# Halves of three kinds of loads as issue entries of their own, and a new issue table, in a chunked recurrence with a feed-forward layer on one core

## The chip, the core and the metric

The kernel runs on one core of a Trainium2 chip. The core has five engines with instruction streams of their own: TensorE (PE, matmuls; its weight loads are shown as PEld), VectorE (DVE), ScalarE (ACT), GpSimd (POOL) and SyncE (SP), which here only issues DMA transfers. The metric is the device time of one execution in microseconds (us); the median of three executions is given.

## What is computed

For 4 batches and 8 heads a 40 x 40 state runs over 768 time steps; the outputs of all heads are joined to rows of 320 and go through a normalised two-layer feed-forward block.

```python
def _attn_ref(r, k, v, w, a, b):          # each (4, 8, 768, 40)
    for t in range(S):
        y[:, :, t] = einsum('bhd,bhde->bhe', rt, state)
        Sa = einsum('bhde,bhe->bhd', state, at)
        state_decay = state * wt[:, :, None, :] - einsum('bhd,bhe->bhde', Sa, bt)
        state = state_decay + einsum('bhd,bhe->bhde', vt, kt)

def _moe_ref(x, g_ln, w_ch1, w_ch2):      # x: (4, 768, 320)
    xn = (x - mean) / sqrt(var + 1e-06) * g_ln
    return x + maximum(xn @ w_ch1, 0.0) @ w_ch2
```

## The kernel before

The 768 steps are cut into 24 chunks of 32 steps (C = 32, NCH = 24). Within a chunk the recurrence is turned into matrix products; from chunk to chunk only the state is handed on. Two chunks make a group of the feed-forward block.

For each chunk c the kernel has these steps, named by the label `of` of their entry:

- `load0` (function load_e) loads w and a into the tile wa, of which there are two (c modulo 2); `load1` loads k and b into bk, of which there are seven.
- prep: scans over w on DVE make running products gE (label g, L213) and qE (label q, L222); aT is a times qE, in two halves (L231), on DVE or POOL; kb multiplies bk by gE in place (L246), on DVE or POOL; tri (L272) is a set of 16 products of bk and aT on PE, gk its signed copy (L278). aT and gk go to DRAM (d_a, d_g) and come back in other layouts as x2s.
- invert: the triangular matrices of a slab of two or four chunks are inverted in a row of small steps on DVE or POOL (yi, ytmp), and go through DRAM as d_tt to the tiles tt.
- chain: prh (L461), one or more solves with tt (L477) and st (L523), which makes the next state; DVE and ACT copy the results (x, hv, ub) between them. This is the sequence that runs from chunk to chunk.
- post: `rv` (function post_loads, L574) loads r and v into the tile rvu, of which there are two; ut transposes u on PE and ACT copies it into the same rvu (L592); z (L605) is a product of rvu with itself, y (L625) the output.
- ss (L555) transposes the state for y.
- After every second chunk, norm and moe for the group: l1 (L860), relu on ACT (hh, L865), its remainder on DVE (hl, L869), l2 (L837). Both layers use split-precision operands, three or more matmuls for each product.

No scheduler sets the order. The body only records entries ("tasks"), each with the keys that it reads and writes; a long string, TABLE, then lists their numbers in the order in which they are emitted, with the letter of the engine (p PE, d DVE, a ACT, g POOL, s SP) and, for those that need PSUM, the bank. Each engine runs its entries in that order, and waits at an entry until its data are there or its buffer is free. All DMA transfers are issued by SP, in the table's order, so an entry that waits on SP holds up all transfers behind it. A chunk from the third on is loaded in two halves of 48 partitions (RHALF), by two DMA instructions; in the kernel before, both belong to one entry.

The names that the change touches: load_e and its labels load0 and load1, post_loads and its label rv, the keys ("wa", i), ("bk", i) and ("rv", i) wherever they are read, and TABLE.

## Time and profile before

| | |
|---|---|
| median of three executions | 590.12 us (589.9 to 590.15) |
| the profiled execution | 590.2 us, of which 588.4 us are the span from its first to its last instruction |
| granted clock of PE, mean of what is recorded | 0.96 of full speed |
| busy: PE, DVE, ACT, POOL | 490.8, 420.1, 277.9, 200.5 us |
| read from and written to DRAM | 69.12 MB and 18.24 MB, 148 GB/s over the span |

The span is what the trace covers; 1.8 us of the execution lie around it. A busy time is the sum over the instructions of an engine, whatever limits the stage that they stand in.

### The profile page before, as it was taken

Reading aid. Unit: us, or ns where it says so; the run is one execution under the profiler, and the core shown is the slowest. Engines: PE = TensorE matmul, PEld = TensorE weight load, DVE = VectorE, ACT = ScalarE, POOL = GpSimd, SP = SyncE. Lnnn points to the kernel's source line nnn. Section 1 sums busy time; section 2 is a strip of 40 time slices with the busy share of each in tenths; the row PEclk is TensorE's granted clock in tenths of the full one; section 3 lists DMA queues with packets and bytes.
Section 4 is the critical chain, followed back from the end, with each engine's and each line's share of the span. In section 5 each row is a group of like instructions: output and inputs, shape, how many; then the busy total and the mean of one; then the engine's idle time right before and its main releaser. Section 6 shows DMA issues by size and latency. Waiting matters only on the chain.

```text
span 588.4 us, 24992 instructions
## 1 busy us (share of the span) xinstructions
PE 490.8 (83%) x10786; PEld 446.5 (76%) x10786; DVE 420.1 (71%) x908; ACT 277.9 (47%) x685; POOL 200.5 (34%) x284
## 2 busy tenths in 40 slices
PE   2540468789689889989997989599999999999996
PEld 2530367678579777988896979499999988989995
DVE  8687997788886879768787667477688865464531
ACT  8031745455346545444751555364435457453331
POOL 8433671247813462015523016445246400000000
PEclk9999999999889879989997989799999999999999
DMA  9999886658697699674994846668667747323000
GB/s 217 214 244 260 199 191 198 130 144 166 145 198 139 149 185 210 157 153 127 210 179 97 166 105 163 122 171 190 130 197 198 149 104 167 88 61 73 8 23 27
DMA packets 114387, 89.04 MB, mean 151 GB/s; under 512 B 83616, under 2 KB 94368, under 8 KB 114272
## 3 DMA queue, kind: packets, MB, share of 16 engines
q1 hardware_dynamic: 114272, 87.40, 64.5%
q8 instruction: 86, 1.41, 1.1%
q14 instruction: 29, 0.24, 0.1%
HBM read 69.12 MB, written 18.24 MB: 148 GB/s over the span
## 4 chain that ended last, share of the span: by engine, by line
PE 62%; DMA 14%; DVE 10%; issue 4%; ACT 3%; POOL 3%; SPq 3%; ACTq 0%; POOLq 0%; DVEq 0%
PE ps L860 18%; PE ps L837 17%; DMA wa<-in_et_dram 4%; PE ps L605 4%; DMA rvu<-in_rv_dram 4%; DMA bk<-in_et_dram 4%; PE ps L477 3%; PE ps L272 3%; PE ps L625 3%; PE ps L523 3%; PE ps L461 2%; PE ps L432 2%; PE ps L555 2%; DVE aT L231 2%; PE ps L586 1%
## 5 line engine op out<-in xcount | busy, mean ns | idle before, releaser
L837 PE MATMUL ps<-w,hh 128*128 128x320 f32 x480 | 118.9, 333 | 0.6 <-ACT xk L440 0.4
L860 PE MATMUL ps<-xh,w 128*128 128x256 f32 x480 | 110.4, 292 | 1.6 <-DVE w L751 1.0
L368 POOL TENSOR_TENSOR ytmp<-yi 128x198 f32<-128x198 f32 (+14 forms) x94 | 61.3, 652 | 93.1 <-DVE yi L372 83.2
L865 ACT ACTIVATE hh<-ps 128x256 fp32r<-128x256 f32 x120 | 45.5, 384 | 98.1 <-PE ps L860 92.1
L869 DVE SCALAR_TENSOR_TENSOR hl<-ps,hh 128x256 fp32r<-128x256 f32 x120 | 49.3, 419 | 54.1 <-ACT hh L865 53.3
L860 PEld LDWEIGHTS ps<-xh,w 128*128 128x128 f32 x480 | 84.4, 194 | 4.0 <-DVE w L751 1.3
L837 PEld LDWEIGHTS ps<-w,hh 128*128 128x128 f32 x480 | 79.8, 196 | 3.9 <-issue 0.5
L837 PE MATMUL ps<-w,hl 128*128 128x320 f32 x240 | 76.4, 318 | 0.0
L860 PE MATMUL ps<-xl,w 128*128 128x256 f32 x240 | 68.7, 286 | 0.0
L372 POOL TENSOR_TENSOR yi<-yi,ytmp 128x198 f32<-128x198 f32 (+19 forms) x104 | 58.8, 565 | 8.2
L231 POOL TENSOR_TENSOR aT<-wa,qE 48x512 f32<-48x512 f32 x23 | 28.4, 1236 | 72.2 <-PE ps L272 23.7
L440 ACT COPY xk<-ps 64x320 f32<-64x320 f32 x96 | 39.4, 419 | 20.8 <-PE ps L432 19.7
L837 PEld LDWEIGHTS ps<-w,hl 128*128 128x128 f32 x240 | 47.0, 196 | 0.1
L860 PEld LDWEIGHTS ps<-xl,w 128*128 128x128 f32 x240 | 46.6, 194 | 0.0
L272 PE MATMUL ps<-aT,bk 104*64 104x64 f32 x768 | 37.4, 271 | 9.0 <-ACT pi L263 5.7
L564 ACT COPY xk<-ps 40x320 f32<-40x320 f32 x92 | 38.4, 420 | 13.0 <-PE ps L555 11.8
L272 PEld LDWEIGHTS ps<-aT,bk 104*64 104x64 f32 x768 | 33.8, 181 | 12.6 <-issue 10.5
L613 DVE TENSOR_TENSOR x5s<-ps,mask 64x512 f32<-64x512 f32 x48 | 33.0, 687 | 14.1 <-PE ps L605 13.3
L213 DVE TENSOR_TENSOR_SCAN gE<-wa,start 112x528 f32<-112x528 f32 x24 | 30.4, 1267 | 14.6 <-DMA wa<-in_et_dram 14.5
L477 PEld LDWEIGHTS ps<-hv,tt 32*32 32x32 f32 (+1 forms) x1536 | 26.8, 121 | 14.8 <-issue 8.2
L508 ACT COPY x<-ps 32x320 f32<-32x320 f32 x62 | 25.9, 418 | 25.1 <-DVE x L508 13.8
L477 PE MATMUL ps<-hv,tt 32*32 32x40 f32 (+1 forms) x1536 | 30.3, 213 | 8.8 <-issue 3.1
(131 smaller groups left out, 1004.3 us busy)
## 6 DMA issues: line engine op xcount, KB each, us to landing
rvu<-in_rv_dram SPq DMA_DIRECT2D x48, 288.0 KB, 5.2
wa<-in_et_dram SPq DMA_DIRECT2D x44, 195.2 KB, 4.7
bk<-in_et_dram SPq DMA_DIRECT2D x44, 192.0 KB, 4.6
d_g<-gk SPq DMA_DIRECT2D x48, 128.0 KB, 3.1
x<-in_vt_dram SPq DMA_DIRECT2D x48, 128.0 KB, 3.6
d_a<-aT SPq DMA_DIRECT2D x48, 99.0 KB, 3.5
x2s<-d_a SPq DMA_DIRECT2D x48, 99.0 KB, 3.3
x5s<-in_r_dram SPq DMA_DIRECT2D x48, 96.0 KB, 3.1
```

The costliest lines, as they stand in the source:

```text
L231: (nc.gpsimd if e == "POOL" else nc.vector).tensor_tensor(out=a[rs, x, :, 0:256].rearrange("p x (i t) -> p i x t", t=C), in0=t[rs, 529:104 ...
L272: nc.tensor.matmul(banks[b[f"pg{c}"]][64 * pp:64 * pp + 64, 64 * i:64 * i + 64], lhsT=tb[R4, 64 * p:64 * p + 64], rhs=a[R4, :, pp, C * i:C ...
L368: g.tensor_tensor(out=tv, in0=y[:, j + 1:, j:j + 1].broadcast_to([n, m, j]), in1=y[:, j:j + 1, 0:j].broadcast_to([n, m, j]), op=ALU.mult)
L372: g.tensor_tensor(out=yv, in0=yv, in1=tv, op=ALU.add)
L440: nc.scalar.copy(out=xk[c % 2][zs, pp, :, hf], in_=banks[b[names[hf]]][zs, 0:CH].rearrange("p (j e) -> p j e", e=D))
L477: nc.tensor.matmul(o[xs, h], lhsT=lhs, rhs=vec[xs, h], start=True, stop=True)
L564: nc.scalar.copy(out=xk[i][bs, pp, par::2].rearrange("p h f e -> p f h e"), in_=banks[b[name]][64 * par:64 * par + D, 0:CH].rearrange("p ( ...
L613: nc.vector.tensor_tensor(out=x5s[zs, pp].rearrange("p f h t -> p (f h) t"), in0=banks[b[f"pz{c}"]][zs].rearrange("p (n t) -> p n t", t=C) ...
L837: nc.tensor.matmul(banks[b[name]][:, 0:CH], lhsT=l[:, us], rhs=ws[f"w2_{f}"][:, y], start=f == 0 and x == 0, stop=f == 9 and x == 2)
L860: nc.tensor.matmul(ph, lhsT=l, rhs=r, start=x == 0, stop=x == 7)
L865: nc.scalar.activation(out=hhs[n], in_=banks[b[name]][:, 0:256], func=AF.Relu)
L869: nc.vector.scalar_tensor_tensor(out=hls[n], in0=banks[b[name]][:, 0:256], scalar=0.0, in1=hhs[n].bitcast(F32), op0=ALU.max, op1=ALU.subtract)
```

## The change

Each half of a load of w and a, of k and b, and of r and v becomes an entry of its own, with a key of its own; whoever reads such a tile now names both halves. The loads of the first two chunks, which are made in one piece, stay one entry. The table is a new one throughout: it lists 2,669 entries in place of 2,601, in a new order, gives some of them to other engines (kb: 15 of 24 on DVE in place of 11; the halves of aT: 27 of 48 on POOL in place of 23), and takes other PSUM banks. The transfers are the same in number, size and address, and so are the matmuls.

```diff
     def load_e(c, part):
         t, cs, k = ((wa[c % 2], slice(0, 1041), ("wa", c % 2)), (bk[c % NBK], slice(1041, 2065), ("bk", c % NBK)))[part]
 
-        def emit():
-            for rs in RHALF if c > 1 else (R,):
-                sync.dma_start(out=t[rs], in_=et_in[c, rs, cs])
-        dma(emit, 380 if c > 1 else 430, w=[k], of=f"load{part}")
+        for x, rs in enumerate(RHALF if c > 1 else (R,)):
+            dma(lambda rs=rs: sync.dma_start(out=t[rs], in_=et_in[c, rs, cs]), 195 if c > 1 else 430,
+                w=[k + (x,)] + ([k + (1,)] if c < 2 else []), of=f"load{part}")
...
-        task("DVE", g_, 1.4, r=[kw, ks], w=[kg], of="g")
+        task("DVE", g_, 1.4, r=kws + [ks], w=[kg], of="g")
...
-        task("PE", tri, 0.75, r=[kbk, ("aT", c % 2, 0), ("aT", c % 2, 1)], bank=f"pg{c}", of="tri")
+        task("PE", tri, 0.75, r=kbs + [("aT", c % 2, 0), ("aT", c % 2, 1)], bank=f"pg{c}", of="tri")
...
-        def rv_():
-            for x, rs in enumerate(RHALF):
-                sync.dma_start(out=rvu[i][rs, 512 * x:512 * x + 1536], in_=rv[c, rs])
-        dma(rv_, 590, w=[("rv", i)], of="rv", land=3.0)
+        for x, rs in enumerate(RHALF):
+            dma(lambda x=x, rs=rs: sync.dma_start(out=rvu[i][rs, 512 * x:512 * x + 1536], in_=rv[c, rs]), 295,
+                w=[("rv", i, x)], of="rv", land=3.0)
...
-        task("ACT", vu_, 0.62, ps=[f"put{c}"], w=[("vu", i)], of="ut")
+        task("ACT", vu_, 0.62, r=[("rv", i, 0), ("rv", i, 1)], ps=[f"put{c}"], w=[("vu", i)], of="ut")
...
-        task("PE", z, 0.75, r=[("rv", i), ("vu", i)], bank=f"pz{c}", of="z")
+        task("PE", z, 0.75, r=[("rv", i, 0), ("rv", i, 1), ("vu", i)], bank=f"pz{c}", of="z")
...
 TABLE = """
-9d 26a 17g 29s 47s 22g 2d 30s 16a 99s 5d 96s 15g 3d 14d 516s 64d 28a 21g 48s 31d 4g 23g 10a 32d 33d 19g 18a 49d 6g 12a
+2d 13a 8g 29s 47s 0d 5d 99s 14d 4g 9d 20g 7g 311s 96s 31d 30s 312s 23g 32d 33d 22g 49d 38a 24g 526s 27a 527s 35d 510s
```

The first place is on SP, at the rv load of chunk 3 (tile rvu1); bk4 is the k and b load of a later chunk, wa1 a w and a load, r1 a weight load. Before:

```order
L194 DMA bk4_89<-in_et_dram 48x1024 x2
L578 DMA x5s_96<-in_r5_dram 48x512
L303 DMA d_g3_171<-gk_110 64x512 x2
L405 DMA x2_0_92<-in_vt_dram 32x1024
L578 DMA x5s_96<-in_r5_dram 48x512
L194 DMA wa1_84<-in_et_dram 48x1041 x2
L574 DMA rvu1_102<-in_rv_dram 48x1536 x2
```

and in the changed kernel:

```order
L304 DMA d_g3_171<-gk_110 64x512 x2
L193 DMA bk4_89<-in_et_dram 48x1024 x2
L663 DMA r1_0_3_1897<-in_w1_dram 128x256
L574 DMA rvu1_102<-in_rv_dram 48x1536
L193 DMA wa1_84<-in_et_dram 48x1041
```

The bk load now stands behind the d_g store, one half of the rv load stands behind bk and one weight load, and its other half stands some twenty rows further ahead, outside this piece; the wa load stands behind it in two entries.

The second place is on SP, at the rv load of chunk 14 (tile rvu0), from a tt load on; rvu1 is that of chunk 15, d_a21 a store of aT. Before:

```order
L398 DMA x2s_0_94<-d_a16_160 48x2x264
L310 DMA d_a21_165<-aT1_109 48x528 x2
L398 DMA x2s_0_94<-d_a16_160 48x2x264
L401 DMA x2s_1_95<-d_g4_172 32x2x256
L401 DMA x2s_0_94<-d_g5_173 32x2x256
L398 DMA x2s_1_95<-d_a15_159 48x2x264
L194 DMA wa1_84<-in_et_dram 48x1041 x2
L574 DMA rvu1_102<-in_rv_dram 48x1536 x2
L398 DMA x2s_1_95<-d_a15_159 48x2x264
L574 DMA rvu0_101<-in_rv_dram 48x1536 x2
L405 DMA x2_1_93<-in_vt_dram 32x1024
L194 DMA wa0_83<-in_et_dram 48x1041 x2
```

and in the changed kernel:

```order
L412 DMA tt0_115<-d_tt4_179 32x8x32 x4
L399 DMA x2s_0_94<-d_a16_160 48x2x264
L578 DMA x5s_96<-in_r5_dram 48x512
L412 DMA tt1_116<-d_tt4_179 32x8x32 x4
L574 DMA rvu0_101<-in_rv_dram 48x1536
L311 DMA d_a21_165<-aT1_109 48x528 x2
L574 DMA rvu0_101<-in_rv_dram 48x1536
L574 DMA rvu1_102<-in_rv_dram 48x1536
L578 DMA x5s_96<-in_r5_dram 48x512
L193 DMA wa0_83<-in_et_dram 48x1041
```

The two halves for chunk 14 now stand ahead of that for chunk 15. The load of wa1 stands further ahead, outside this piece, in two entries, and so do three of the x2s loads; the other two x2s loads come later.

The third place is on POOL, at the two kb products (line L246, L247 in the changed kernel) on bk5 and bk4, which follow a row of inversion steps. Before:

```order
L368 TENSOR_TENSOR ytmp0_113<-yi0_111 128x130
L372 TENSOR_TENSOR yi0_111<-yi0_111,ytmp0_113 128x5x26
L231 TENSOR_TENSOR aT0_108<-wa0_83,qE0_105 48x8x2x32
L246 TENSOR_TENSOR bk5_90<-bk5_90,gE1_104 112x1024
L246 TENSOR_TENSOR bk4_89<-bk4_89,gE0_103 112x1024
L336 MEMSET yi1_112 128x32
L368 TENSOR_TENSOR ytmp1_114<-yi1_112 128x30
L372 TENSOR_TENSOR yi1_112<-yi1_112,ytmp1_114 128x30
```

and in the changed kernel:

```order
L373 TENSOR_TENSOR yi0_111<-yi0_111,ytmp0_113 128x2x29
L369 TENSOR_TENSOR ytmp0_113<-yi0_111 128x30
L373 TENSOR_TENSOR yi0_111<-yi0_111,ytmp0_113 128x30
L232 TENSOR_TENSOR aT0_108<-wa0_83,qE0_105 48x8x2x32 x2
L247 TENSOR_TENSOR bk4_89<-bk4_89,gE0_103 112x1024
L337 MEMSET yi1_112 128x32
```

The product on bk5 is no longer on POOL (it is on DVE, some way ahead), and both halves of aT0 stand ahead of the one on bk4; before, one of these halves was on POOL and the other on DVE.

## Rows read from the trace of the kernel before

**Rows 1.** The page: busy us (share of the span) xinstructions of each engine.
```profile
PE 490.8 (83%) x10786; PEld 446.5 (76%) x10786; DVE 420.1 (71%) x908; ACT 277.9 (47%) x685; POOL 200.5 (34%) x284
```

**Rows 2.** Stages: length, busy of PE, PEld, DVE, ACT, POOL, clock, DMA share, GB/s.
```profile
0.00:60.00 60.00, 20.26 (x500) 17.56 (x500) 45.67 (x84) 20.64 (x37) 30.75 (x34) 1.00 0.93 233
...
136.00:156.50 20.50, 14.53 (x413) 12.75 (x412) 17.30 (x32) 9.62 (x26) 17.15 (x21) 0.99 0.77 174
...
136.00:380.00 244.00, 212.60 (x4923) 191.09 (x4924) 183.76 (x392) 120.24 (x303) 94.80 (x136) 0.91 0.73 158
...
380.00:550.00 170.00, 169.28 (x3965) 156.57 (x3963) 113.02 (x261) 85.94 (x219) 39.49 (x60) 1.00 0.56 134
```

**Rows 3.** PE's timeline: start, us, instruction, idle before it and its releaser.
```profile
157.04 1.98 PE L605 MATMUL ps<-rvu 104*64 104x64 f32 x32 [3.83 <-ACT rvu L592]
...
254.04 0.27 PE L477 MATMUL ps<-hv,tt 32*32 32x40 f32 x7 [1.71 <-issue]
...
314.95 1.30 PE L523 MATMUL ps<-x,xk 64*40 64x40 f32 x64 [4.26 <-ACT x L508]
...
376.26 0.92 PE L555 MATMUL ps<-ident,x 40*104 40x40 f32 x16 [6.79 <-ACT rvu L592]
```

**Rows 4.** Stages, as in rows 2: the stretches after three of the waits.
```profile
156.50:163.30 6.80, 6.01 (x119) 5.36 (x120) 6.21 (x13) 3.49 (x10) 3.52 (x7) 0.52 0.46 108
313.50:320.30 6.80, 5.35 (x82) 5.25 (x83) 3.60 (x8) 1.56 (x4) 0.00 (x0) 0.52 0.50 102
374.90:381.80 6.90, 5.54 (x86) 5.02 (x90) 2.92 (x6) 4.20 (x9) 0.10 (x1) 0.52 0.26 60
```

**Rows 5.** PE's timeline: two places before 136 us and one after.
```profile
111.42 1.98 PE L605 MATMUL ps<-rvu 104*64 104x64 f32 x32 [0.52 <-ACT rvu L592]
...
132.34 0.92 PE L523 MATMUL ps<-x,xk 64*40 64x40 f32 x21 [1.25 <-DVE x L508]
...
342.60 1.15 PE L605 MATMUL ps<-rvu 104*64 104x64 f32 x32
```

**Rows 6.** SP's timeline, 142 to 149 us: start, us, DMA issue, how many.
```profile
142.67 0.78 SPq L194 DMA_DIRECT2D bk<-in_et_dram  x2
...
148.99 0.89 SPq L574 DMA_DIRECT2D rvu<-in_rv_dram  x2
```

**Rows 7.** The chain that ended last: its pieces for two rv loads (start, us).
```profile
149.46 6.79 DMA rvu<-in_rv_dram
...
366.49 9.03 DMA rvu<-in_rv_dram
```

**Rows 8.** SP's timeline, 359 to 366 us.
```profile
359.05 0.39 SPq L398 DMA_DIRECT2D x2s<-d_a  x1
...
363.68 0.89 SPq L194 DMA_DIRECT2D wa<-in_et_dram  x2
...
366.02 2.18 SPq L574 DMA_DIRECT2D rvu<-in_rv_dram  x2
```

**Rows 9.** Stages, as in rows 2: 370 to 375 us.
```profile
370.00:375.00 5.00, 0.00 (x0) 0.00 (x0) 0.69 (x2) 0.00 (x0) 3.02 (x5) 0.96 1.04 192
```

**Rows 10.** The page's DMA issues: how many, KB each, median us to landing.
```profile
rvu<-in_rv_dram SPq DMA_DIRECT2D x48, 288.0 KB, 5.2
```

**Rows 11.** DVE's and POOL's timelines from 309 us.
```profile
309.00 4.93 DVE L231 TENSOR_TENSOR aT<-wa,qE 48x512 f32<-48x512 f32 x1
...
309.04 4.34 POOL L246 TENSOR_TENSOR bk<-bk,gE 112x1024 f32<-112x1024 f32 x2
```

**Rows 12.** Line L231: its instructions on DVE, duration in ns min/median/max.
```profile
L231 DVE TENSOR_TENSOR aT<-wa,qE x25: 651/690/4930, 9.7 to 403.4; 48x512 f32<-48x512 f32 x25
```

**Rows 13.** Groups by line on DVE: kb, busy us, mean ns, idle before.
```profile
L246 DVE TENSOR_TENSOR bk<-bk,gE 112x1024 f32<-112x1024 f32 x11 | 13.7, 1246 | 0.2
```

**Rows 14.** SP's and DVE's timelines in the start.
```profile
68.07 1.89 SPq L411 DMA_DIRECT2D tt<-d_tt  x4
...
57.61 1.26 DVE L213 TENSOR_TENSOR_SCAN gE<-wa,start 112x528 f32<-112x528 f32 x1 [3.64 <-DMA wa<-in_et_dram]
```

More of the change, by code (lines that the diff above doesn't have):

```diff
@@ L190, in load_e @@
         t, cs, k = ((wa[c % 2], slice(0, 1041), ("wa", c % 2)), (bk[c % NBK], slice(1041, 2065), ("bk", c % NBK)))[part]
-        def emit():
-            for rs in RHALF if c > 1 else (R,):
-                sync.dma_start(out=t[rs], in_=et_in[c, rs, cs])
-        dma(emit, 380 if c > 1 else 430, w=[k], of=f"load{part}")
+        for x, rs in enumerate(RHALF if c > 1 else (R,)):
+            dma(lambda rs=rs: sync.dma_start(out=t[rs], in_=et_in[c, rs, cs]), 195 if c > 1 else 430,
+                w=[k + (x,)] + ([k + (1,)] if c < 2 else []), of=f"load{part}")
     def prep(c):
         t, tb = wa[c % 2], bk[c % NBK]
-        kw, kbk = ("wa", c % 2), ("bk", c % NBK)
+        kws = [("wa", c % 2, x) for x in range(2)]
+        kbk = ("bk", c % NBK)
+        kbs = [kbk + (x,) for x in range(2)]
         n = 528
@@ L224, in q_ @@
                 initial=0.0, op0=ALU.mult, op1=ALU.max)
-        task("DVE", q_, 1.31, r=[kw, "last"], w=[kq], of="q")
+        task("DVE", q_, 1.31, r=kws + ["last"], w=[kq], of="q")
         a = aT[c % 2]
@@ L234, in a_ @@
                     in1=qe[rs, :, 1:33].rearrange("p (i x) t -> p i x t", x=2), op=ALU.mult)
-            task([("DVE", 0.68), ("POOL", 1.18)], a_, r=[kw, kq], w=[("aT", c % 2, x)], of="aT")
+            task([("DVE", 0.68), ("POOL", 1.18)], a_, r=kws + [kq], w=[("aT", c % 2, x)], of="aT")
         if c < 2 or c in FRAME:
@@ L247, in kb_ @@
                 out=kb, in0=kb, in1=ge[R, :, 0:C].unsqueeze(2).broadcast_to([112, 16, 2, C]), op=ALU.mult)
-        task([("DVE", 1.25), ("POOL", 2.2)], kb_, r=[kg], w=[kbk], of="kb")
+        task([("DVE", 1.25), ("POOL", 2.2)], kb_, r=[kg], w=kbs, of="kb")
         def qd_(e, b):
@@ L434, in pe @@
                         identity=ident[rs, rs])
-        task("PE", pe, 0.65, r=[("bk", c % NBK), "ident"], bank=names, of="kbt")
+        task("PE", pe, 0.65, r=[("bk", c % NBK, x) for x in range(2)] + ["ident"], bank=names, of="kbt")
         for hf in range(2):
@@ L927, in setup @@
         for i in range(2, NBK):
-            clear(bk[i][32:64], [("bk", i)], ("POOL",))
+            clear(bk[i][32:64], [("bk", i, 0), ("bk", i, 1)], ("POOL",))
         clear(ub, ["ub"])
@@ L931, in setup @@
         for i in range(2):
-            clear(rvu[i], [("rv", i), ("vu", i)])
+            clear(rvu[i], [("rv", i, 0), ("rv", i, 1), ("vu", i)])
     setup()
@@ L946, in range_check @@
     def range_check():
-        key = ("bk", NCH % NBK)
+        key = ("bk", NCH % NBK, 0)
+        both = [key, ("bk", NCH % NBK, 1)]
         acc = bk[NCH % NBK]
@@ L953, in zero @@
             (nc.gpsimd if e == "POOL" else nc.vector).memset(v, 0)
-        task([("POOL", 1.0), ("DVE", 0.6)], zero, w=[key], of="wz")
+        task([("POOL", 1.0), ("DVE", 0.6)], zero, w=both, of="wz")
         for i in range(8):
             t = wa[i % 2]
-            dma(lambda i=i, t=t: sync.dma_start(out=t[:, 0:n], in_=ww[i]), 492, w=[("wa", i % 2)], of="ww")
+            dma(lambda i=i, t=t: sync.dma_start(out=t[:, 0:n], in_=ww[i]), 492, w=[("wa", i % 2, 0), ("wa", i % 2, 1)], of="ww")
             def wild(e, b, t=t):
@@ L962, in wild @@
                     op0=ALU.bitwise_xor, op1=ALU.bitwise_or)
-            task("DVE", wild, 1.2, r=[("wa", i % 2)], w=[key], of="wild")
+            task("DVE", wild, 1.2, r=[("wa", i % 2, 0), ("wa", i % 2, 1)], w=[key], of="wild")
         def fold(e, b):
@@ L1202 @@
[L1202 to L1205 removed]
+2d 13a 8g 29s 47s 0d 5d 99s 14d 4g 9d 20g 7g 311s 96s 31d 30s 312s 23g 32d 33d 22g 49d 38a 24g 526s 27a 527s 35d 510s
+6g 34d 21g 50d 309s 97a 39p0 51d 36a 131a1 54a 64g 295s 37d 28a 310s 48s 10g 53d 41p2 52d 19a 292s 16a 293s 91p34 42d
@@ new lines @@
+781d 1009g 779a 1352d 985a 784p 1338d 680p5 879s 679p7 788d 1345s 685p 786d 1010g 787d 773s 881s 785d 986p4 801s
+1342p1 1353d 987a 968a 686p4 798a 1369d 1339a 803p2 1343d 1355g 1386a 804a 1370d 899p31 682a 1354d 805p2 900a 1371d
+1382s 791a 886p0 1057s 880s 806d 1011g 887a 1344s 807d 888p0 884s 1373d 684p 890a 1383s 808p2 1012d 901a 891a 1013d
+893a 911s 1356a 912s 913p3 683d 687a 1014g 1364s 809d 892a 689p 903a 812d 690p 1029s 889a 904p62 1015d 1028s 902a
+1056s 696p0 1016d 905a 1385s 914a 1384s 1372d 908a 915p1 1387d 906a 907a 1361p3 1166s 916d 1017g 1025s 894p62 917d
@@ L1206 @@
+2648s 2645d 2646s
 """
```

253 lines of the change are left out of this document (125 added, 128 removed).

## The prediction

> **What bounds the kernel now.** The page comes first: TensorE (PE) is busy for 490.8 of 588.4 us [rows 1], and the change takes no matmul away, so only PE's idle time and its clock can give anything back. The table by stage says where the idle time lies [rows 2]. From 0 to 60 us PE works 20.3 us while the DMA engines are 93% busy: that stage is bound by transfers. From 136 to 380 us PE works 212.6 of 244 us; 31 us of idle are there. From 380 to 550 us it works 169.3 of 170 us: it is the bound. A microsecond that PE gains before 380 therefore reaches the end of the kernel, since the work behind it is already packed.
>
> The timeline of PE is read next, for those 31 us. Three waits stand out: 3.83, 4.26 and 6.79 us, at 157, 315 and 376 us, 14.9 us together [rows 3]. The rest are shorter waits behind other engines, and pauses that the profile puts on nothing but "issue", of which the row at 254 us is one of five between 196 and 343 us, each 1.2 to 2.1 us and some 8 us together. Those five belong to the instruction stream of PE, which keeps its 644 entries, so I leave them as they are.
>
> Each long wait has a second price. After it the granted clock falls: 0.52 in the three stretches that hold these waits, hence nearly all at 1.2 GHz, and 1.00 around them, 2.4 GHz [rows 4]. The same 32 matmuls take 1.98 us at the one and 1.15 us at the other [rows 5]. PE works 6.01, 5.35 and 5.54 us in the three stretches, 16.9 us, of which about half, 8.45 us, would not be needed at the upper level. The rows also show that the lower level held at 111 us, where the profile prints no fall: its clock records begin at 136 us, and until about there the matmuls have the long duration.
>
> The Trainium skill speaks against the second price: "TensorE: Matmul & The Clock Gate", in "Wait — 56ns, not 53.3ns?" and the section on what is happening, counts the slow start of matmuls as under 1% of a typical span and advises not to fit it. By that all falls of this kernel together would cost at most 5.9 us, and the forecast below would be an estimated 583.3 us in place of 582.4. The rows give more for three falls alone, and I go by the rows.
>
> **What makes the three waits.** At 157 us PE's z product (L605) waits for ACT, and ACT for the rv load of chunk 3. In SP's queue the bk load goes out at 142.67 us [rows 6]; the rv load stands behind five more entries, the last of them a wa load, goes out at 148.99, and is on its way for 6.79 us [rows 7]. At 376 us it is the rv load of chunk 14: SP issues the first entry of that run at 359.05, reaches the wa load at 363.68 and this rv load only at 366.02 us [rows 8]; it lands after 9.03 us [rows 7], while the DMA engines are 1.04 busy and PE does nothing from 370 to 375 us [rows 9], against a median of 5.2 us for this load [rows 10]. At 315 us no load is late: one aT product on DVE takes 4.93 us [rows 11], against a median of 0.69 us [rows 12], exactly while POOL runs two kb products one behind the other, 4.34 us, and a copy that the chain waits for stands behind it.
>
> **The change, part by part.**
>
> Halving: the halves were two DMA instructions before, and are two now. Nothing is added to SP, and the number of waits for a consumer is the same, since every reader names both halves. Cost: 0. What hides it is that a half which waits holds up only what is queued behind it, as the pair did. Without that cover, one half behind a busy buffer would delay its neighbours by its wait; I bound that with the 0.89 us that a pair takes to issue [rows 6].
>
> First wait, rv of chunk 3: one half now goes out long before, and the second stands behind bk and one weight load. At 0.45 us an issue (0.89 for two, [rows 6]) it is out about 1.3 us after bk, in place of 6.3 us: 5.0 us sooner, more than the 3.83 us of wait. 256 KB of the weight go between in place of some 970 KB. Gain 3.83 us.
>
> Third wait in time, rv of chunk 14: from the first x2s load of the run to the rv load there were 1.6 MB of other loads and 6.97 us of issue. Now there are 0.4 MB and four entries, some 4.5 us by 0.45 us for a plain issue and 1.89 us for a tt load of four pieces [rows 14]: 2.5 us less. Of the 1.2 MB that no longer lie in the run, 0.7 MB come later, worth 3.8 us at the 192 GB/s of that stretch [rows 9]; the rest, mostly the load of wa1, was moved further ahead and may or may not be through by then, 2.2 us. Together 6.3 to 8.5 us against a wait of 6.79 us: it goes but for half a microsecond at most, and I count all of it. Next to be late there would be the load of wa0 behind it.
>
> Second wait, kb on POOL: the pair is taken apart, one of the two products goes to DVE, and both aT halves of the next chunk go to POOL ahead of the other. The aT that was held is no longer on DVE there. Gain 4.26 us. DVE pays 1.25 us for a kb [rows 13]; it is busy 184 of 244 us there [rows 2], so this lies in its idle time. Without that cover, it would be 1.25 us for each of the four kb that DVE takes over in all, 5 us.
>
> The start: the first tt load, from which the chain of solves begins, is issued at 68.07 us [rows 14]. By the sizes of the issues 15.4 MB stand ahead of it before, 15.2 MB now. At 233 GB/s [rows 2] that is 66 us and 65 us. I take 0. On DVE a scan waited 3.64 us for wa ahead of the last step of the inversion [rows 14]; with its own 1.26 us it bounds a gain at 4.9 us. The bound on the other side is as much.
>
> New waits: some 2,670 entries stand in a new order, and the old one had three long waits that its author surely did not want. Below, none; above, four. I take two, at the mean price of the old three, (14.88 + 8.45) / 3 = 7.8 us: two of the old three came from queued loads, which the new order treats with care at both places that I can follow, and one from DVE and POOL, which it does not.
>
> **Sum.** The profiled execution took 590.2 us, 0.1 above the median of the three runs: 588.4 of span and 1.8 around it. 590.2 - 14.88 - 8.45 + 15.6 = 582.4 us.
>
> **Rivals.**
>
> *Everything is gained.* No new long wait, and the start shorter by up to 4.9 us: 590.2 - 23.3 = 566.9, down to 562. For it: the packed stage from 380 us shows that PE can run for 170 us with under 1 us of idle. Against it: nothing in rows says that a list of this length holds no surprise like the 4.93 us product. Chance 0.12.
>
> *New waits eat it all, or halving does nothing.* Both halves are needed by the same reader, and the bytes are the same; if other loads become the late ones, three waits of 7.8 us return: 590 us, with 588 to 592 around it. DVE now has more products with two operands in SBUF, and POOL more aT: a wait of the kind at 315 us could come back anywhere, at up to 4.26 us each with its clock. "SBUF — State Buffer", "Who interferes with whom", of the Trainium skill, says that such a DVE instruction and a POOL instruction that reads SBUF exclude each other for the whole instruction; the 4.93 us agree with it. Chance 0.14.
>
> *Slower: the clock rises later.* PE runs at the lower level until about 136 us. Shortly ahead of the rise there is a wait of 1.25 us at 132.34 us [rows 5]; if the new order has one more in that stretch, 117 to 136 us, the rise may come only after the wait at 157 us did. PE's 14.53 us of work between 136 and 156.5 us [rows 2] would then be done at the lower level, for 14.5 us more: 596.9 us with the rest as forecast, 604.7 us if nothing else is gained. It decides as soon as the added cost exceeds the 7.8 us that the sum gains. For it: the same three engines feed PE there, and the order is new. Against it: a sequence of PE that reads nearly the same up to there. Chance 0.22.
>
> **Numbers.** The forecast, 573 to 588 us, gets 0.52. A measurement of this kernel tells about 0.2%, 1.2 us, from no change. Faster: 0.52 + 0.12 + a quarter of the second rival, 0.67. Within 0.2%: half of the second rival, 0.08 rounded up. Slower: the third rival and what is left of the second, 0.25. The range for 8 in 10 reaches into the first and the third rival: 568 to 595 us. The likeliest case alone is 573 to 588 us.
>
> **What would show it.** Right: no idle of more than 2 us on PE ahead of L605 or of the transposes at L556 (L555 before) with "ACT rvu" as releaser; rv loads of chunks 3 and 14 landed before ACT's copy at L592 comes up; no aT on DVE above 2 us; fewer stretches at the lower clock after 136 us; a stage at the end that is still packed. Wrong: a new wait of 4 us or more after 136 us, of whatever releaser; 32 matmuls of L605 that still take 1.98 us after 140 us; a first tt issue later than 70 us.

## The result, and the profile after

The changed kernel took 579.7 us, the median of four executions (572.7, 576.7, 582.7 and 582.8), against 590.0 us (589.9 to 590.2). The ratio is 0.9741 (95%: 0.9684 to 0.9798), 15.3 us; it leaves the two executions above 582 us out, which the comparison counts as disturbed, and by the mean of all four (578.7 us) it would be 11.3 us. Two later comparisons gave 0.983 and 0.981, 10 and 11 us (below). The profiled execution is the shortest of the four, 572.7 us with a span of 571.0.

The page's busy row, the row of its DMA queue for instructions and its row of rv loads, which answer to [rows 1, 10]:

```profile
PE 480.7 (84%) x10786; PEld 435.5 (76%) x10786; DVE 412.9 (72%) x892; ACT 281.5 (49%) x693; POOL 195.8 (34%) x292
...
q8 instruction: 86, 1.41, 1.1%
...
rvu<-in_rv_dram SPq DMA_DIRECT2D x48, 288.0 KB, 4.9
```

PE works 10.1 us less on the same 10,786 matmuls, and stands idle for 90.3 us in place of 97.6. The table by stage of the changed kernel (columns as in [rows 2]), with the three stretches of [rows 4]:

```profile
0.00:60.00 60.00, 20.86 (x468) 18.12 (x468) 48.05 (x85) 27.61 (x50) 24.70 (x38) 1.00 0.99 227
136.00:380.00 244.00, 219.65 (x5395) 196.67 (x5396) 188.46 (x415) 130.02 (x331) 103.43 (x149) 0.97 0.77 170
380.00:550.00 170.00, 166.05 (x3541) 154.54 (x3541) 108.45 (x253) 80.11 (x201) 25.51 (x42) 1.00 0.52 117
156.50:163.30 6.80, 6.07 (x136) 5.44 (x134) 6.14 (x18) 2.81 (x10) 2.43 (x5) 1.00 0.75 162
313.50:320.30 6.80, 6.67 (x124) 6.11 (x120) 6.31 (x10) 2.39 (x7) 0.00 (x0) 1.00 0.47 115
374.90:381.80 6.90, 6.90 (x184) 6.53 (x183) 4.76 (x15) 4.48 (x12) 0.92 (x3) 1.00 0.50 137
```

The middle stage has 24 us of idle in place of 31, the three stretches run at 2.4 GHz (clock 1.00), and the stage from 380 us on, which had 0.7 us of idle, now has 4. PE's timeline of the changed kernel, at the places of [rows 3, 5] (z of chunks 2, 3 and 14, the transposes of chunk 14) and at its three longest pauses after 136 us:

```profile
130.34 1.15 PE L605 MATMUL ps<-rvu 104*64 104x64 f32 x32
...
148.47 1.48 PE L605 MATMUL ps<-rvu 104*64 104x64 f32 x32
...
260.24 0.97 PE L433 MATMUL ps<-ident,bk 40*128 40x40 f32 x15 [3.53 <-issue]
...
300.60 0.41 PE L837 MATMUL ps<-w,hl 128*128 128x320 f32 x1 [2.62 <-issue]
...
353.31 0.60 PE L556 MATMUL ps<-ident,x 40*104 40x40 f32 x16
...
357.41 1.15 PE L605 MATMUL ps<-rvu 104*64 104x64 f32 x32
...
371.04 0.37 PE L860 MATMUL ps<-xl,w1x 128*128 128x256 f32 x1 [2.27 <-issue]
```

No named wait of more than 1.7 us is left after 136 us; what is left is named "issue". To see where the 17.4 us of the two spans went, both kernels are cut at the same work: up to z of chunk 0, of chunk 4, of chunk 14, and the end. Before:

```profile
0.00:88.10 88.10, 35.21 (x764) 30.98 (x764) 71.80 (x133) 37.29 (x78) 51.23 (x69) 1.00 0.90 221
88.10:188.40 100.30, 84.11 (x1736) 74.80 (x1736) 79.86 (x182) 53.12 (x135) 41.95 (x62) 0.95 0.71 160
188.40:383.40 195.00, 173.07 (x4130) 155.31 (x4122) 144.73 (x303) 92.91 (x233) 69.47 (x96) 0.91 0.71 155
383.40:588.40 205.00, 198.41 (x4167) 185.46 (x4166) 123.67 (x293) 94.62 (x240) 37.86 (x59) 0.99 0.47 114
```

and in the changed kernel:

```profile
0.00:85.20 85.20, 35.60 (x764) 31.17 (x764) 69.31 (x124) 40.91 (x83) 41.90 (x71) 1.00 0.96 219
85.20:177.50 92.30, 80.22 (x1736) 69.95 (x1736) 78.35 (x178) 51.88 (x134) 47.98 (x65) 0.93 0.79 174
177.50:357.40 179.90, 163.06 (x4117) 146.17 (x4117) 137.21 (x287) 95.22 (x240) 70.99 (x100) 0.97 0.77 169
357.40:571.00 213.60, 201.85 (x4178) 188.24 (x4169) 128.02 (x305) 93.52 (x237) 34.96 (x57) 0.99 0.48 112
```

Length less PE's busy time is the idle time. The changed kernel is ahead by 2.9 us at chunk 0, 10.9 at chunk 4 and 26.0 at chunk 14, and gives 8.6 us back behind it. Its idle time differs by -3.3, -4.1, -5.1 and +5.2 us in the four parts, its busy time by +0.4, -3.9, -10.0 and +3.4. The loss at the end belongs to the new order and not to this one execution. The last part of a second profile of the changed kernel (after_again), and that of a kernel with the old order from chunk 3 on (h_af2), both described below:

```profile
366.12:575.50 209.38, 200.24 (x4176) 186.56 (x4169) 128.16 (x305) 93.43 (x237) 34.96 (x57) 0.99 0.49 114
369.68:574.60 204.92, 198.49 (x4167) 185.46 (x4166) 123.65 (x293) 94.62 (x240) 37.96 (x59) 1.00 0.48 113
```

In the nine profiles with the old order and all loads there, the last part takes 204.9 to 209.3 us; in two of the changed kernel 209.4 and 213.6.

### The profile page after: what moved, and what is told of

Read it like the earlier page. It is cut to its first block, busy times and chain, and to the rows that moved or that the text cites. A ratio compares the mean times of both kernels' runs of the same rounds, so it can differ in the third digit from the quotient of the medians.

```text
span 571.0 us, 24966 instructions
## 1 busy us (share of the span) xinstructions
PE 480.7 (84%) x10786; PEld 435.5 (76%) x10786; DVE 412.9 (72%) x892; ACT 281.5 (49%) x693; POOL 195.8 (34%) x292
## 4 chain that ended last, share of the span: by engine, by line
PE 62%; DMA 14%; DVE 10%; issue 6%; POOL 3%; SPq 2%; ACT 2%; DVEq 0%; POOLq 0%
PE ps L860 19%; PE ps L837 17%; DMA wa<-in_et_dram 6%; PE ps L605 3%; PE ps L478 3%; PE ps L625 3%; DMA x5s<-in_r_dram 3%; PE ps L273 3%; PE ps L462 2%; PE ps L556 2%; PE ps L524 2%; PE ps L433 2%; DVE gE L214 2%; PE ps L586 2%; DMA x<-in_vt_dram 2%
## 5 line engine op out<-in xcount | busy, mean ns | idle before, releaser
L837 PE MATMUL ps<-w,hh 128*128 128x320 f32 x480 | 115.7, 326 | 0.4 <-ACT ub L515 0.4
L369 POOL TENSOR_TENSOR ytmp<-yi 128x150 f32<-128x150 f32 (+13 forms) x95 | 60.0, 632 | 90.1 <-DVE yi L373 85.7
L837 PEld LDWEIGHTS ps<-w,hh 128*128 128x128 f32 x480 | 78.1, 192 | 5.6 <-issue 2.9
L373 POOL TENSOR_TENSOR yi<-yi,ytmp 128x210 f32<-128x210 f32 (+16 forms) x108 | 61.6, 571 | 8.5
L273 PE MATMUL ps<-aT,bk 104*64 104x64 f32 x768 | 35.9, 263 | 23.3 <-POOL bk L247 15.1
L232 POOL TENSOR_TENSOR aT<-wa,qE 48x512 f32<-48x512 f32 x27 | 34.3, 1269 | 62.0 <-DVE qE L223 34.1
L273 PEld LDWEIGHTS ps<-aT,bk 104*64 104x64 f32 x768 | 32.3, 174 | 27.4 <-POOL bk L247 16.1
L565 ACT COPY xk<-ps 40x320 f32<-40x320 f32 x92 | 38.6, 420 | 12.9 <-PE ps L556 11.2
L214 DVE TENSOR_TENSOR_SCAN gE<-wa,start 112x528 f32<-112x528 f32 x24 | 31.8, 1323 | 11.2 <-POOL bk L247 5.4
L860 PE MATMUL ps<-xl,w1x 128*128 128x256 f32 x120 | 33.9, 283 | 2.3 <-issue 2.3
```

What stands on the lines that cost most here:

```text
L214: nc.vector.tensor_tensor_scan(out=flat(ge[R]), data0=t[R, 0:n], data1=flat(st_[R]), initial=0.0, op0=ALU.mult, op1=ALU.max)
L232: (nc.gpsimd if e == "POOL" else nc.vector).tensor_tensor(out=a[rs, x, :, 0:256].rearrange("p x (i t) -> p i x t", t=C), in0=t[rs, 529:104 ...
L273: nc.tensor.matmul(banks[b[f"pg{c}"]][64 * pp:64 * pp + 64, 64 * i:64 * i + 64], lhsT=tb[R4, 64 * p:64 * p + 64], rhs=a[R4, :, pp, C * i:C ...
L369: g.tensor_tensor(out=tv, in0=y[:, j + 1:, j:j + 1].broadcast_to([n, m, j]), in1=y[:, j:j + 1, 0:j].broadcast_to([n, m, j]), op=ALU.mult)
L373: g.tensor_tensor(out=yv, in0=yv, in1=tv, op=ALU.add)
L565: nc.scalar.copy(out=xk[i][bs, pp, par::2].rearrange("p h f e -> p f h e"), in_=banks[b[name]][64 * par:64 * par + D, 0:CH].rearrange("p ( ...
```

## Experiments

A ratio is to the kernel before in the same comparison; "us less" is what the ratio lacks of 1, times 590 us, with its 95% interval. The kernel before varied more in the later comparisons (medians 588.8 to 592.7 us, executions 585 to 601) than in the first, so a difference of 1.2 us, which the prediction took to be telling, is too small to tell there.

### The three late waits alone

In the kernel before, each of the three waits of [rows 3] was taken out by one edit, and then all three. The rv load of chunk 14 (b_rv14), in SP's queue:

```diff
 L411 DMA tt_115<-d_tt_179 32x8x32 x4
+L574 DMA rvu_101<-in_rv_dram 48x1536 x2
 L398 DMA x2s_94<-d_a_160 48x2x264
...
 L398 DMA x2s_95<-d_a_159 48x2x264
-L574 DMA rvu_101<-in_rv_dram 48x1536 x2
 L405 DMA x_1_93<-in_vt_dram 32x1024
```

> The kernel before, with one edit: the rv load of chunk 14 is issued right behind the first tt load of its run, ahead of the two x2s loads, the d_a store and the loads of wa1 and of chunk 15. Theory (a long wait is worth itself and half of the PE work in the slow stretch behind it): the wait of 6.79 us goes and with it half of the 5.54 us of PE work at the lower clock, 2.8 us, so 590.1 - 9.6 = 580.5 us. Rival 1 (what is gained is given back in short pauses behind it, since the stage from 380 us on has no room): the wait goes, the time falls by 2 to 6 us only, and the pauses named issue grow from the 8.4 us of before. Rival 2 (loads that it is moved past, x2s or wa1, become the late ones): a wait of 3 us or more within 20 us of the old place, 586 us or more.

The rv load of chunk 3 (b_rv3), in SP's queue:

```diff
 L194 DMA bk_89<-in_et_dram 48x1024 x2
+L574 DMA rvu_102<-in_rv_dram 48x1536 x2
 L578 DMA x5s<-in_r_dram 48x512
...
 L194 DMA wa_84<-in_et_dram 48x1041 x2
-L574 DMA rvu_102<-in_rv_dram 48x1536 x2
```

> The kernel before, with one edit: the rv load of chunk 3 is issued right behind the bk load that stood five entries ahead of it. Theory: the wait of 3.83 us goes and half of the 6.01 us of PE work at the lower clock behind it, 3.0 us: 590.1 - 6.8 = 583.3 us. Rival 1 (given back later, in part by the wait of 4.26 us near 315 us that stays): 586 to 588 us. Rival 2 (the clock does not stay up there for another reason, since other falls follow at 173 and 197 us without a long wait): 590.1 - 3.8 = 586.3 us with a granted clock near 157 us that is still about 0.5.

The aT product that ran on DVE beside POOL's kb (b_at), on POOL:

```diff
-L231 TENSOR_TENSOR aT_108<-wa_83,qE_105 48x8x2x32
+L231 TENSOR_TENSOR aT_108<-wa_83,qE_105 48x8x2x32 x2
 L246 TENSOR_TENSOR bk_90<-bk_90,gE_104 112x1024
```

> The kernel before, with one edit of one letter: the second half of aT of chunk 19 runs on POOL, behind the first half and ahead of the two kb products, in place of DVE. Theory: DVE has no aT beside POOL's kb, the copy that the chain waits for comes at once, the wait of 4.26 us goes and half of the 5.35 us of PE work at the lower clock, 2.7 us: 590.1 - 7.0 = 583.1 us. Rival 1 (POOL's products now end 1.2 us later, and DVE's scan or copy beside them is held as aT was): another DVE instruction of over 2 us between 309 and 316 us, 588 us or more. Rival 2 (given back behind it at the wait for rv of chunk 14, which is there in any case): the wait at 376 us grows from 6.79 to 9 us or more and the time falls by less than 4 us.

All three edits in one kernel (b_three):

> The kernel before with the three edits together, no halves and otherwise the old order. Theory (three waits and their clock, 14.88 + 8.45 us, add up): 590.1 - 23.3 = 566.8 us, less than the 572.7 us of the changed kernel's profiled execution, so that the new table brings nothing that the three edits do not. Rival 1 (gains are given back in pauses named issue, as in the changed kernel, where these rose from 8.4 to 18.1 us): 574 to 578 us, with no wait above 2 us and 15 us or more of such pauses. Rival 2 (the changed kernel's gain came from its start and earlier clock, and the waits are refilled): 583 us or more.

| | ratio | us less | priced in the sum |
|---|---|---|---|
| b_rv14 | 0.9932 (0.9897 to 0.9968) | 4.0 (1.9 to 6.1) | 9.6 |
| b_rv3 | 0.9989 (0.9943 to 1.0035) | 0.6 (-2.1 to 3.4) | 6.8 |
| b_at | 0.9884 (0.9800 to 0.9968) | 6.8 (1.9 to 11.8) | 7.0 |
| b_three | 0.9846 (0.9781 to 0.9911) | 9.1 (5.3 to 12.9) | 23.3 |

PE's timeline of b_rv14, where the wait of chunk 14 was:

```profile
375.06 0.60 PE L555 MATMUL ps<-ident,x 40*104 40x40 f32 x15 [2.11 <-DVE hl L869]
```

PE's timeline of b_rv3, where the wait of chunk 3 was:

```profile
154.06 1.98 PE L605 MATMUL ps<-rvu 104*64 104x64 f32 x32 [1.43 <-ACT start L208]
```

and of b_three at the same place:

```profile
157.37 1.94 PE L605 MATMUL ps<-rvu 104*64 104x64 f32 x31 [4.67 <-issue]
```

and of b_at, at the state product that had waited 4.26 us:

```profile
305.07 0.83 PE L523 MATMUL ps<-x,xk 64*40 64x40 f32 x64
```

Each wait goes. Behind the two loads another stands: a product on DVE, another copy on ACT, and with all three edits a pause of 4.67 us named issue in the place of the load of chunk 3. Taking out the wait of chunk 3 alone gains nothing that can be measured; the 32 matmuls there still take 1.98 us, the lower clock. Behind the wait for aT nothing stands, and this edit alone is worth its price, within a wide interval. The interval of b_three (5 to 13 us) excludes 23 us.

### The changed kernel again

No edit.

> The changed kernel as it is, beside the kernel before on one chip, to see how much its time and granted clock vary. Theory (the size of the gain hangs on TensorE's clock, whose first lasting rise came at 128.9 us in the profiled execution, and later in others): the times spread over 8 us or more, and go with the granted clock, about 5 us for each 0.02 of it (572.7 us at 0.974, 576.7 at 0.960, 582.7 at 0.934). Rival (the spread is in transfers, the clock only follows the waits): the PE idle differs between profiled executions by as much as the time does, with PE busy within 3 us of 480.7 us.

> The changed kernel as it is, as a measure for the three runs beside it: 9 to 12 us below the kernel before on the same chip, as in the two earlier comparisons (medians 579.7 against 590.0 us and 578.8 against 588.8 us).

Ratios 0.9829 (0.9786 to 0.9872) and 0.9814 (0.9690 to 0.9938): 10.1 (7.6 to 12.6) and 11.0 us less (3.7 to 18.3). The six executions of the first stand in nearly the order of their granted clock, 575.3 us at 0.976, 577.3 at 0.979, 578.3 at 0.957, 579.3 at 0.949, 580.9 and 582.7 at 0.939, as the theory has it; in the profiled one PE was busy for 483.0 us, within 3 us of 480.7, as the rival has it. The kernel before shows no such order there (587.5 us at 0.970, 587.2 at 0.929), nor do the five executions of the second, so the mean of the clock does not explain a time by itself.

### Halves side by side

In the changed kernel both halves were put side by side at the place of the later one (a_late) or of the earlier one (a_early), and then at the later place those of r,v alone (a_rv) and those of w,a and k,b alone (a_wb). Two of the rv loads in a_rv:

```diff
-L574 DMA rvu_102<-in_rv_dram 48x1536
...
-L574 DMA rvu_102<-in_rv_dram 48x1536
+L574 DMA rvu_102<-in_rv_dram 48x1536 x2
 L193 DMA bk_86<-in_et_dram 48x1024
...
 L663 DMA r_0_3_1896<-in_w_dram 128x256
-L574 DMA rvu_102<-in_rv_dram 48x1536
+L574 DMA rvu_102<-in_rv_dram 48x1536 x2
 L193 DMA wa_84<-in_et_dram 48x1041
```

> The changed kernel with both halves of each of the three kinds of loads side by side, at the place of the later half; the rest of its table as it is. Theory (the new order of the other entries made the gain, halving made nothing): within 3 us of the changed kernel, no wait above 3 us behind a load after 136 us. Rival 1 (halving matters, since a half that stands far ahead, by 30 and 35 entries for chunks 0 and 1 and 9 and 23 for chunks 2 and 3, lands in time only so): z of chunks 0 to 3 starts 2 to 5 us later and the end is 4 us or more later. Rival 2 (pairs are better): 3 us or more faster.

> The changed kernel with both halves side by side at the place of the earlier half (the run with the later place took 595.9 us against 578.8 us, with 26.0 us of pauses named issue after 160 us in place of 16.6). Theory (two halves in a row are one larger burst, behind which PE's next block of instructions comes late, wherever the pair stands): 588 us or more, with 22 us or more of such pauses after 160 us. Rival 1 (what cost 17 us was the later place of the first halves, not the pairs): within 4 us of the changed kernel's 578.8 us, and such pauses of 14 to 19 us. Rival 2 (the loads that the second half now passes become late): a named wait of 3 us or more behind a load after 136 us.

> The changed kernel with only the halves of r,v side by side, at the place of the later half (all three kinds there cost 17 us). Theory (what the halves bring is a half of r,v issued long ahead: these stand up to 35 entries apart, and each is 288 KB): 10 us or more of the 17 us are lost, 588 us or more where the changed kernel takes 579 us. Rival (the loads of w,a and k,b, for whose tiles the next chunk's scans wait, are the ones): within 4 us of the changed kernel.

> The changed kernel with only the halves of w,a and of k,b side by side, at the place of the later half. Theory (the r,v halves carry the gain): within 4 us of the changed kernel. Rival (w,a and k,b carry it): 10 us or more slower than the changed kernel, with pauses named issue of 22 us or more after 160 us.

a_late: 1.0097 (1.0042 to 1.0151), 5.7 us more than the kernel before. a_rv: 1.0051 (1.0010 to 1.0092), 3.0 us more. a_wb: 0.9818 (0.9741 to 0.9896), level with the changed kernel. So with the r,v halves at the later place the whole gain is gone, and the halves of the other two kinds bring nothing measurable. a_early, 0.9834 (0.9734 to 0.9935), is level with the changed kernel by this ratio, though its median lies only 3.3 us below the kernel before; as far as it goes, it says that the late place is what costs, not the pair. Behind the start PE waits by name for none of the three kinds of loads for over 0.7 us in a_rv; its longest wait for any load there is one of 2.32 us for x5s. PE's timeline of a_rv at its two longest pauses:

```profile
270.04 0.63 PE L433 MATMUL ps<-ident,bk 40*128 40x40 f32 x14 [3.90 <-issue]
...
388.60 0.37 PE L860 MATMUL ps<-xl,w1x 128*128 128x256 f32 x1 [4.05 <-issue]
```

and a_rv cut at the same work as the two kernels above:

```profile
0.00:86.02 86.02, 35.60 (x764) 31.18 (x764) 68.29 (x124) 40.90 (x83) 41.15 (x71) 1.00 0.93 217
86.02:182.67 96.65, 84.02 (x1736) 73.47 (x1736) 78.54 (x179) 52.13 (x134) 47.78 (x65) 0.86 0.72 163
182.67:373.03 190.36, 169.81 (x4117) 152.16 (x4118) 137.03 (x287) 95.49 (x240) 70.22 (x100) 0.93 0.74 159
373.03:594.40 221.37, 205.09 (x4176) 191.15 (x4169) 127.96 (x305) 93.55 (x237) 34.99 (x57) 0.97 0.50 110
```

At chunk 4 a_rv stands at 182.7 us, beside 177.5 and 181.7 in the two profiles of the changed kernel and 188.4 before; at chunk 14 at 373.0, beside 357.4, 366.1 and 383.4; and at the end at 594.4, beside 571.0, 575.5 and 588.4. Most of what the later place costs is therefore lost behind chunk 4, and it is lost most of all in the last part.

One try to draw 14 more pairs apart (a_apart), in SP's queue:

```diff
-L193 DMA bk_89<-in_et_dram 48x1024 x2
+L193 DMA bk_89<-in_et_dram 48x1024
+L193 DMA bk_87<-in_et_dram 48x1024
 L193 DMA bk_90<-in_et_dram 48x1024
+L193 DMA bk_89<-in_et_dram 48x1024
```

> The changed kernel in which 14 more pairs of halves that stand within three entries of each other are drawn apart: the first half of eight pairs goes up to four entries of SP's queue ahead, the second half of six pairs two entries back. Theory (smaller bursts, fewer late blocks of instructions for PE): the pauses named issue fall below 16 us and the time by 1 to 4 us, 575 to 578 us. Rival (a half moved back is late, or one moved ahead delays a load that is waited for): a new named wait of 2 us or more after 136 us, 580 us or more.

0.9770 (0.9705 to 0.9834), 13.6 us less (9.8 to 17.4), level with the changed kernel within the intervals: inconclusive.

### Old start, new rest, and the reverse

The first 617 entries, through z of chunk 3, in the old order and the rest in the new (h_bf); 650 entries in the new order, which reach into chunk 3, and the rest in the old (h_af); and the second with two of the edits above (h_af2), which stand there as

```diff
 L412 DMA tt_115<-d_tt_179 32x8x32 x4
+L574 DMA rvu_101<-in_rv_dram 48x1536 x2
 L399 DMA x2s_94<-d_a_160 48x2x264
...
-L232 TENSOR_TENSOR aT_108<-wa_83,qE_105 48x8x2x32
+L232 TENSOR_TENSOR aT_108<-wa_83,qE_105 48x8x2x32 x2
```

> The changed kernel, in which the first 617 entries stand in the order and on the engines of the kernel before (through z of chunk 3, some 157 us; halves side by side there, two loads of chunk 9 the last of them), and all that follows in the order of the changed kernel; four PSUM banks are renamed where the two orders meet. Theory (6 us of the gain were made before 150 us, by an earlier start of the chain and an earlier clock): z of chunk 3 starts at 154 to 157 us and the end is 5 to 9 us later than that of the changed kernel. Rival (the start brought nothing that lasts, as the later stages are bound by other things): z of chunk 3 as late, but the end within 3 us of the changed kernel's.

> The start of the changed kernel (its first 650 entries, through z of chunk 2 and most of chunk 3) with the order and the engines of the kernel before from there on, whose halves stand side by side; six PSUM banks are renamed where the two orders meet. The other mixture, old start and new rest, took 586.2 us against 578.8 us of the changed kernel and 588.8 us of the kernel before. Theory (the start is worth the 7.4 us that the other mixture lost): z of chunk 3 starts at 148 to 153 us and the time is 581 to 583 us. Rival 1 (the gains of the two parts do not add, since an early start is given back at the old waits at 315 and 376 us, which then grow): 585 us or more, with a wait of over 6 us ahead of the transposes of chunk 14. Rival 2 (the start brings nothing by itself): 588 us or more, z of chunk 3 as late as in the kernel before.

> The mixture of new start and old rest (3.1 us below the kernel before), with the two edits to the old rest: the rv load of chunk 14 ahead of its run, and the second half of aT of chunk 19 on POOL. Theory (the start's gain and the removed waits add up, and are the whole of the change): 9 to 12 us below the kernel before, level with the changed kernel within 3 us. Rival (the rest of the new table, with its halves, brings something of its own): 4 us or more above the changed kernel, with no named wait above 3 us after 160 us to explain it.

h_bf: 0.9910 (0.9846 to 0.9973), 5.3 us less (1.6 to 9.1). h_af: 0.9891 (0.9841 to 0.9941), 6.4 us less (3.5 to 9.4; by the mean of all its executions, 588.8 against 593.2 us, 4.4), though the two later old waits are still there and one has grown; that of chunk 3 is gone. PE's timeline of h_af:

```profile
314.50 1.30 PE L524 MATMUL ps<-x,xk 64*40 64x40 f32 x64 [4.03 <-ACT x L509]
...
376.10 0.92 PE L556 MATMUL ps<-ident,x 40*104 40x40 f32 x16 [8.23 <-ACT rvu L592]
```

and its stages up to z of chunk 0 and of chunk 4:

```profile
0.00:86.35 86.35, 35.82 (x764) 31.31 (x764) 68.94 (x124) 40.90 (x83) 40.96 (x71) 1.00 0.96 217
86.35:187.59 101.24, 87.44 (x1736) 77.13 (x1736) 78.16 (x177) 53.52 (x136) 47.81 (x68) 0.90 0.79 168
```

PE is idle for 4.8 us less up to there than before (7.4 us less in the changed kernel), but works 3.9 us more, so that this profile, of one of the longer executions (591.1 us), is only 0.9 us ahead at chunk 4.

h_af2: 0.9684 (0.9599 to 0.9769), 18.6 us less (13.6 to 23.7); its median is 575.7 us, beside 586.4 of the changed kernel and 591.5 of the kernel before on that chip. The new start (6.4) and the two edits (4.0 and 6.8) make 17.2 us: within the intervals they add up. I had expected 9 to 12 us; the result beats both kernels without the rest of the new table. It keeps the old order's last part, 204.9 us.

Two waits of the first solves, behind DVE's w1x and hv, are in every profile with the old start. With the new start neither stands there by those names; in the changed kernel's profile the first solve waits for its tt load. Before, and in the changed kernel:

```profile
74.06 2.02 PE L477 MATMUL ps<-hv,tt 64*64 64x40 f32 x32 [2.87 <-DVE w1x L737]
81.24 1.93 PE L477 MATMUL ps<-hv,tt 64*64 64x40 f32 x32 [2.72 <-DVE hv L488]
...
72.59 2.10 PE L478 MATMUL ps<-hv,tt 64*64 64x40 f32 x32 [1.78 <-DMA tt<-d_tt]
```

Two moves on DVE were to take the two waits out of the kernel before (b_start), and with the three edits (b_four):

```diff
+L737 TENSOR_TENSOR w1x<-ps_68,w1x 64x320 x2
 L222 SCALAR_TENSOR_TENSOR qE_105<-wa_83,last 112x528
-L737 TENSOR_TENSOR w1x<-ps_68,w1x 64x320 x2
...
+L488 TENSOR_TENSOR hv_99<-ps_68,hv_99 128x320
 L705 TENSOR_TENSOR ps_67<-ps_67,r_1_575 128x320
...
-L488 TENSOR_TENSOR hv_99<-ps_68,hv_99 128x320
```

> The kernel before with two moves on DVE in the start: one preparation of w1x ahead of the scan at 71.6 us, and the copy hv of the first solve ahead of three steps on weights at 78.7 us. Theory (what the start gained is DVE's order, and the copies of the first solves no longer stand behind the preparation of weights): the waits of 2.87 and 2.72 us fall by 1.3 and 2.0 us, z of chunk 0 comes 3 us sooner, and the time falls by 3 to 7 us, a part of it by an earlier clock. Rival (the start is bound by transfers, and what DVE gives back is waited for at tt, x2s or wa): z of chunks 1 to 3 less than 1 us sooner, and the time within 1.5 us of the kernel before.

> The kernel before with the two moves on DVE in the start and the three edits at the late waits (these three alone: 9.1 us less). Theory (four places make up the change): 12 to 16 us less than the kernel before, level with the changed kernel, whose three comparisons gave 10.1 to 15.3 us. Rival 1 (the new start gains by its transfers, not by DVE's order): 8 to 10 us less, no better than the three edits. Rival 2 (gains are given back at pauses named issue): 10 us or more of pauses beyond the 16.5 us of the three edits.

0.9979 (0.9941 to 1.0017) and 0.9869 (0.9815 to 0.9924), 1.2 (-1.0 to 3.5) and 7.7 us less (4.5 to 10.9): the moves bring nothing that can be measured. PE's timeline of b_start:

```profile
73.04 2.02 PE L477 MATMUL ps<-hv,tt 64*64 64x40 f32 x32 [2.34 <-DVE w1x L737]
...
79.31 1.93 PE L477 MATMUL ps<-hv,tt 64*64 64x40 f32 x32 [1.80 <-DVE hv L488]
...
84.86 1.73 PE L523 MATMUL ps<-x,xk 64*40 64x40 f32 x64 [1.71 <-ACT x L508]
```

The two waits shrink by 0.5 and 0.9 us only, where 1.3 and 2.0 were expected, and a new one of 1.71 us stands behind them. So the moves did not do what they were to do, and DVE's order is neither shown as the cause nor excluded.

### Fewer loads

Both kernels leave out the three kinds of loads of chunks 10 to 23 (a_fewer, b_fewer), and their products run on what the tiles held; in the changed one:

```diff
-            dma(lambda x=x, rs=rs: sync.dma_start(out=rvu[i][rs, 512 * x:512 * x + 1536], in_=rv[c, rs]), 295,
+            dma(lambda x=x, rs=rs: sync.dma_start(out=rvu[i][rs, 512 * x:512 * x + 1536], in_=rv[c, rs]) if c < 10 else None, 295,
```

> The changed kernel without the loads of w,a, of k,b and of r,v of chunks 10 to 23, 19 MB of 69; the products run on what the tiles held. Theory (the pauses named issue are PE waiting for its next block of instructions, 86 transfers of 16 KB in a queue of their own, and come late when many loads are under way): of the 14 us of such pauses after 200 us less than 5 us stay, and the time falls by 8 us or more. Rival 1 (such a pause is a matter of PE's own stream: as many instructions, as many pauses): 12 us or more of them stay, and the time falls by less than 4 us. Rival 2 (loads still set the pace after 200 us by named waits): pauses stay, and named waits of DMA or of ACT behind rvu are what goes.

> The kernel before without the loads of w,a, of k,b and of r,v of chunks 10 to 23, 19 MB of 69, as it was left out of the changed kernel in the run that took 556.7 us; the products run on what the tiles held. Theory (the changed kernel's gain after chunk 10 is in how transfers stand, both the late loads and PE's instructions behind them; its start is worth 7 us for itself): 561 to 566 us, so that 5 to 9 us of the difference of 10 us or more between the two stay, without the waits for rvu of chunk 14; the wait at 315 us stays, since no load makes it. Rival (the order of the other entries made the gain): 568 us or more, the difference between the two kernels as large as with all loads.

a_fewer: 0.9457 (0.9413 to 0.9502), 32.0 us less than the kernel before. b_fewer: 0.9606 (0.9523 to 0.9690), 23.2 us less, 571.3 us. The distance of the two, 9 us, is as large as with all loads; the intervals leave 3 to 15 us, so this does not part the theories. The wait that no load makes stays in b_fewer, as both had it:

```profile
308.41 0.95 PE L523 MATMUL ps<-x,xk 64*40 64x40 f32 x64 [4.27 <-ACT x L508]
```

What a_fewer does show is the pauses. The idle time of PE behind z of chunk 4, summed over its timeline, in us:

| | named issue | all others |
|---|---|---|
| kernel before | 8.0 | 14.0 |
| b_three | 9.3, and 7.2 before chunk 4 | 6.9 |
| changed kernel, two profiles | 18.1, 16.6 | 5.0, 5.8 |
| a_late, a_rv | 26.0, 25.2 | 4.3, 6.0 |
| a_fewer | 7.8 | 2.5 |
| b_fewer | 6.5 | 10.2 |
| h_af2 | 9.6 | 9.7 |

In the changed kernel the same instructions of PE with 19 MB less to load have less than half of the pauses. In the kernel before the same cut takes them from 8.0 to 6.5 us only, so fewer loads take away about what the new order adds, and little more.

## Why the direction was right and the size wrong

**The bound, and the three waits.** Right: the waits are gone, z of chunks 3 and 14 stands unbroken, no aT on DVE takes over 2 us after 136 us (one in the start takes 3.48), and the three stretches run at 2.4 GHz.

**Waits and new waits together.** The sum gave the waits and their clock 23.3 us and took 15.6 us back, 7.8 us net. The three edits alone measure 9.1 us (5.3 to 12.9), and the new order behind the start alone 5.3 us (h_bf, 1.6 to 9.1), so the net holds within the intervals. Its two parts do not hold as they were told, and that they came out near the right net is luck: what comes back is not two long waits at 7.8 us but ten pauses named issue of 0.8 to 3.5 us after 160 us; these pauses grow from 8.0 to 18.1 us behind chunk 4 while named waits fall from 14.0 to 5.0. I had left such pauses "as they are", since PE's stream keeps its entries.

**The failing step: "The start ... I take 0."** It was judged by the bytes ahead of the first tt load, which indeed goes out as before (67.87 us against 68.07). But in the old order PE waits at the first solves for DVE, 2.87 and 2.72 us, and not for that load. The new start by itself is worth 6.4 us (3.5 to 9.4). It reaches into chunk 3, so the load of chunk 3 is in it, whose wait alone returned 0.6 us. With the net of the waits, 7.8 us, that makes 14.2 us where 15.3 were measured in the first comparison; with the 5.3 us measured for the rest it makes 11.7, where the later comparisons measured 10.1 and 11.0. The size was missed by 7.5 us in the first comparison and by 2 to 3 in the others, and the start is the term that was missing. In the profiles it is idle time: 7.4 us less up to z of chunk 4 in the changed kernel, 4.8 us less in h_af. It is not an earlier clock: the 32 matmuls of chunk 2 take 1.15 us, the upper level, in both orders, at 130.34 us in the new one and in the old at

```profile
136.46 1.15 PE L605 MATMUL ps<-rvu 104*64 104x64 f32 x32
```

The third rival had the right place, and the wrong sign. What in the new start does it is open: the two moves on DVE shrank the waits there too little to tell, and transfers in the start were not tried apart.

**"A microsecond that PE gains before 380 therefore reaches the end"** does not hold for the new order either: of the 26.0 us that the changed kernel is ahead at chunk 14, 8.6 are lost behind it, where PE is idle for 11.8 us in place of 6.6. The sign "a stage at the end that is still packed" failed. With the old order there, h_af2 keeps what it has gained.

**Halving at 0** was wrong as well, if the place of the halves is counted with it: with the r,v halves side by side at the later place the gain is gone (a_rv). That is not the gain of the start, which a_rv still has at chunk 4 (182.7 us against 188.4 before); it is lost later, and pauses named issue grow to 25.2 us from 16.6 and 18.1. That a half may be late without a named wait for it was not in the sum.

**The clock.** Net 2.8 us was forecast; 10.1 us less of PE work was in the first profile, 7.8 in the second. The Trainium skill, "TensorE: Matmul & The Clock Gate", in the section on what is happening, gives under 1% of a span for the slow start of matmuls; the prediction stretched that to every later fall of the clock. So stretched it does not hold here: the two profiles differ from the old order by 1.7% and 1.3% of the span in PE's work on the same matmuls. Even the slow start alone is more here: most of PE's first 76.7 us of work, up to z of chunk 2, has the long durations of the lower level [rows 5]. The size differs between executions: in the profile of a_wb, which is level with the changed kernel in time, PE works 490.9 us, as long as before. I cannot say what sets it.

## What to carry to other kernels

Price a removed wait by taking it out alone, and look at what stands right behind it: here three waits of 14.9 us returned 9 us, the one with nothing behind it its full price, the two for loads, with the next late engine behind them, far less. Read the start as a stage of its own, by what PE waits for there and not by bytes. Check that what is gained early still stands at the end, by cutting both kernels at the same work. And when two orders differ in thousands of places, cut both tables at one point and cross them: two mixtures and two small edits found a kernel 18.6 us faster than the old one.
